# Seven block products for eight in the last chunk's second matrix product

## The chip, the cores and the metric

One core of one Trainium2 chip. The metric is the time of one execution on the device in microseconds (us), the median of several runs. PE is TensorE (its weight loads are shown as PEld), DVE VectorE, ACT ScalarE, POOL GpSimd, SP SyncE.

## The reference

An attention block with polynomial feature maps feeds a two-layer network with an exact GELU:

```python
def phi(x):                                   # r = 8, so 64 features
    a = np.einsum('rd,bhsd->bhsr', S1, x)
    b = np.einsum('rd,bhsd->bhsr', S2, x)
    return np.einsum('bhsi,bhsj->bhsij', a, b).reshape(*x.shape[:-1], r * r)
q_p, k_p = (phi(q), phi(k))                   # q, k, v: 4 batches, 4 heads, 1088 tokens, 32
kv = np.einsum('bhsf,bhsd->bhfd', k_p, v)
z = np.sum(k_p, axis=2)
num = np.einsum('bhsf,bhfd->bhsd', q_p, kv)
den = np.einsum('bhsf,bhf->bhs', q_p, z)[..., None] + 1e-06
x = (num / den).transpose(0, 2, 1, 3).reshape(4352, 128)
h = x @ w_in                                  # w_in: 128 x 2048
g = 0.5 * h * (1.0 + erf(h / np.sqrt(2)))
out = g @ w_out                               # w_out: 2048 x 128
```

All in float32.

## The kernel before

The 4352 tokens (4 batches of 1088) are cut into chunks. Each batch gives two chunks of 512 tokens, numbers 0 to 7; the 64 tokens that remain of each batch make a ninth chunk, number 8 (`NMAIN`), with 256 tokens. The hidden width 2048 is cut into 16 tiles of 128 (`fi`, `NF` = 16).

The program is one list of steps `(n, fi)`, numbered t. In each step `hidden(n, fi)` (L739) multiplies a tile of `w_in` with the chunk's `xT` into one of two banks `h_ps`, and ACT writes the GELU of it (L746) into a `block` tile in SBUF. The chunks 2 to 7 have 16 steps each, and chunk 8 has the last 16, t = 128 to 143. From t = 18 on a hidden product is issued as two matmuls of 64 output rows each, one for each half of the array (`by_halves`); for chunk 8 that holds to fi 4, and later tiles are one full matmul.

The second product, `g @ w_out`, runs some steps behind. For the main chunks it is done by pairs of tiles: with the 2x2 blocks of a pair (two tiles of hidden width by two halves of the tokens, and by two halves of the 128 output columns), seven block products take the place of eight. The block sums of `w_out` that this needs are made once (`channel_sums`, in tiles T[1] to T[4]); those of the tokens for each block of four tiles by POOL (`token_sums`, L790 to L793); the products are issued two at a time, one for each half of the array (`two_products`, L825); and `drain` (L837 to L846) and `combine` (L859, L860) add the seven sums up. `store` then transposes (L887) and writes the rows out by SP's queue.

For chunk 8 the second product has the other orientation: the tokens are the stationary operand, and the result has tokens as rows. `project` (L873) issues two matmuls of 128x128 for each tile, one for each half of its 256 tokens, and adds all 16 tiles up in two work banks (`w_ps`). The tiles fi 0 to 11 follow the hidden products from t = 133 on, two matmuls a step after the first few; the eight matmuls of fi 12 to 15 come last. Then DVE copies the first half and ACT the second (L882), and SP's and ACT's queues store them.

The order on each engine is that of the text: the program adds a dependency from every instruction to the one before it on its engine. What each step issues stands in tables by step: `slots[t]`, `products[t]`, `drains[t]` (the drain of chunk 7 at t = 133) and `done[t]` (its `combine` and `store` at t = 139). In one step the order is drains, hidden product, slots, stores, products.

Working tiles come from pools: "g" is a ring of four tiles of 128x512, free in the last steps; "sums" holds what `drain` writes; `out_bank()` gives one of two `o_ps` banks, in which chunk 7's seven products lie until its drain, `work_bank()` one of the `w_ps`.

Of the kernel before, what the change touches and what calls it, by code (L numbers as in the profile page):

```python
# [8 lines left out]
FP = mybir.dt.float32  # L9
# [7 lines left out]
def kernel(  # L17
# [18 lines left out]
    pe, dve, act, pool, sp = nc.tensor, nc.vector, nc.scalar, nc.gpsimd, nc.sync  # L36
    B, H, S, D = q.shape
# [4 lines left out]
    NF = d_ff // 128  # L42
# [5 lines left out]
    CW = JC * 128  # L48
    G = 128 // 32
    NCH = J // JC  # L50
    C = D + 1
    LAG = 2
    NMAIN = B * NCH
    NB = 4

    USUAL = 8
    NCHUNK = NMAIN + 1
    assert B == 4 and d_model == 128 == H * D == JC * D == 2 * F and H == 4 and REM == 64 and NCH == 2

    big = ctx.enter_context(tc.tile_pool(name="big", bufs=1))  # L60
    att = ctx.enter_context(tc.tile_pool(name="att", bufs=2))
    mlp = ctx.enter_context(tc.tile_pool(name="mlp", bufs=2))
# [8 lines left out]
    def work_bank():  # L71
        return work_banks()[:, 0]
# [7 lines left out]
    def out_bank():  # L80
        return ops.tile([128, CW], FP, name="o_ps")


    by_act, by_dve, by_pool = act.copy, dve.tensor_copy, pool.tensor_copy
# [12 lines left out]
    w_out_sb = [big.tile([128, c1 - c0], FP, name=f"w_out{i}") for i, (c0, c1) in enumerate(pieces)]  # L97
# [96 lines left out]
    for i, (queue, s) in enumerate(((act, S1), (sp, S2))):  # L194
        s, e = words(s)
# [528 lines left out]
    g_of, o_of = {}, {}  # L724

    def w_tile(w, fi):
        i = max(i for i, (c0, c1) in enumerate(pieces) if c0 <= fi * 128)
        at = fi * 128 - CUTS[i]
        return w[i][:, at:at + 128]
# [3 lines left out]
    def hidden(n, fi, by_halves=False):  # L733
        W = width[n]
        ps = first_banks.pop((n, fi)) if (n, fi) in first_banks else hidden_bank()
        w = w_tile(w_in_sb, fi)
        for rows in (slice(0, 64), slice(64, 128)) if by_halves else (slice(0, 128),):
            if (n, fi) not in begun:
                pe.matmul(ps[rows, :W], lhsT=w[:, rows], rhs=xT[n][:, :W], start=True, stop=True)  # L739
        if n < NCH and fi < USUAL:  # L740
            g_of[n, fi] = mlp.tile([128, CW], FP, name="g", bufs=4)
        else:
            if fi % NB == 0:
                blocks[n, fi // NB] = block(FP)
            g_of[n, fi] = blocks[n, fi // NB][:, fi % NB]
        act.activation(out=g_of[n, fi][:, :W], in_=ps[:, :W], func=ACT.Gelu)  # L746
# [13 lines left out]
    T = {}  # L760
# [94 lines left out]
    def combine(n):  # L855
# [6 lines left out]
            dve.tensor_add(out=N[:, 1], in0=N[:, 1], in1=usual[n])  # L862
        return N[:, 1]

    def project(n, fi, parts=range(B // 2), cols=slice(None)):
        first, final = fi == 0, fi == (USUAL if n < NCH else NF) - 1
        if first:
            o_of[n] = out_bank() if n < NMAIN else [work_bank() for i in range(B // 2)]
        g = g_of[n, fi]
        if n == NMAIN:  # L870

            for i in parts:
                pe.matmul(o_of[n][i][:, :128], lhsT=g[:, i * 128:(i + 1) * 128], rhs=w_tile(w_out_sb, fi),  # L873
                          start=first, stop=final)
            return
        pe.matmul(o_of[n][:, cols], lhsT=w_tile(w_out_sb, fi), rhs=g[:, cols], start=first, stop=final)  # L876

    def store(n):
        oT = mlp.tile([128, JC, d_model], FP, name="oT")
        if n == NMAIN:  # L880
            for i, copy, queue in ((0, by_dve, sp), (1, by_act, act)):
                copy(out=oT[:, i, :], in_=o_of[n][i][:, :128])  # L882
                queue.dma_start(out=out.rearrange("(two b s) d -> two b s d", two=2, s=S)[:, i, MAIN:S, :].rearrange("two s d -> s two d"),
                             in_=oT[:, i, :])
            return

        dve.transpose(out=oT.rearrange("p n d -> p (n d)"), in_=combine(n))  # L887
        row = n // NCH * S + n % NCH * CW
        if n < NCH:

            for c in range(d_model // 32):
                to = out[0:MAIN, c * 32:(c + 1) * 32].rearrange("(g t n j) d -> n j t g d", t=32, n=NCH, j=JC)[n]
                o = oT[c * 32:(c + 1) * 32].rearrange("p n (m d) -> p (n m) d", d=32)
                o = o.rearrange("p (g j) d -> j p g d" if n == 0 else "p (j g) d -> j p g d", j=JC)
                for j in range(JC):
                    sp.dma_start(out=to[j], in_=o[j])
            return
        to = out[row:row + CW].rearrange("(t n) d -> t n d", t=32)
        of = oT.rearrange("p n (m d) -> p (n m) d", d=32)
        for at in (slice(0, 16),) if n != NMAIN - 2 else (slice(0, 8), slice(8, 16)):  # L900
            for c in range(d_model // 32):
                sp.dma_start(out=to[:, at, c * 32:(c + 1) * 32], in_=of[c * 32:(c + 1) * 32, at])
# [250 lines left out]
    for t, (n, fi) in enumerate(steps):  # L1153
        if n < NCH and fi < USUAL:
            products[t + LAG].append((project, n, fi))
            if fi == USUAL - 1:
                slots[t + LAG + 1 + 2 * n].append(lambda n=n: take_usual(n))
        elif n == NMAIN:
            at_ = max(t + LAG, (n * NF + 5) if fi < 3 else (n * NF + 6) if fi < 5 else 0)
            if fi < NF - 4:  # L1160
                products[at_].append((project, n, fi))
            if fi == NF - 1:

                products[at_] += [(project, n, NF - f, (i,)) for f, i in ((4, 0), (3, 0), (2, 0), (4, 1), (1, 0), (3, 1),
                                                                          (2, 1), (1, 1))]
                done[at_ + 1].append(n)
        elif fi % NB == NB - 1:
            b = fi // NB
            opens = b == first_block(n)
            late = int(n < NCH or n == NCH and opens)  # L1170
            for later, pairs in ((3, 3), (4, 2), (5, 2)) if opens else ((2, 2), (3, 2), (4, 1), (5, 2)):
                later += late
                for i in range(pairs):
                    products[t + later].append((two_products, n, b, len([p for q in products.values() for p in q
                                                                        if p[:3] == (two_products, n, b)])))
            if b == NF // NB - 1:
                drains[t + 6 + late].append(n)
                done[t + 12].append(n)

    for t in range(len(steps) + LAG):  # L1180
        if t < 4:

            hidden(0, t)
            if t == 0:
                expand_multiply(1, 0)
                w_out[0].fields()
                expand_copy(1, 1)
                expand_multiply(1, 1)
            if t == 1:
                w_out[0].low_words()  # L1190
                w_out[0].exponents()
                w_out[0].finish()
                w_out[1].fields()
            if t == 2:
                w_out[1].low_words()
            if t == 3:
                banks = work_banks()
                numerators_by_token(1, halves(banks), range(JC))
                w_out[1].mantissas(by_pool=True)
                w_out[1].exponents()  # L1200
                divide(1, halves(banks), 0)
                w_out[1].signs()
                w_out[1].product()
                project(0, 0)
                project(0, 1, cols=slice(0, 256))
                turn_half(1, 0, work_bank(), by_act)
                project(0, 1, cols=slice(256, 512))
                turn_half(1, 1, work_bank(), by_dve)
            continue
        if t == 4:  # L1210
            first_hidden(1, 0)
            for f, *a in products[t]:
                f(*a)
            first_hidden(1, 1)
        for n in drains[t]:
            drain(n)
        sooner = t == NMAIN * NF
        if sooner:
            for f, *a in products[t]:
                f(*a)  # L1220
        if t < len(steps):
            n, fi = steps[t]
            hidden(n, fi, by_halves=t >= 18 and (n < NMAIN or fi < 5))
        if t < len(steps) and steps[t][0] < NMAIN and steps[t][1] % NB == NB - 1:
            n, b = steps[t][0], steps[t][1] // NB
            if b >= first_block(n):
                token_sums(n, b)
        for f in slots[t]:
            f()
        for n in done[t]:  # L1230
            store(n)
        if t != 4 and not sooner:
            for f, *a in products[t]:
                f(*a)
# [41 lines left out]
```

## Time and profile before

| | us |
|---|---|
| median of 3 runs | 258.85 (258.77 to 259.4) |
| profiled execution, its own time | 258.97 |
| profiled execution, span from first to last instruction | 257.2 |
| PE busy | 253.0 |
| POOL / DVE / ACT busy | 164.5 / 151.6 / 114.7 |

The page gives busy time and share of each engine, the span in 40 slices, the chain of work that ended last, and the costliest groups of instructions. In the lines of a timeline the columns are start in us, duration in us, engine, line of the kernel, operation, output<-inputs, shape (for PE `128*64` is the size of the stationary operand, rows by columns, and what follows is the moving one), and xN for N merged records; idle time ahead of it and what ended that stand in brackets. A float32 matmul shows as two records. The granted TensorE clock is 1.00 throughout.

### The profile page before, as it was taken

The page shows a single profiled execution, that of the slowest core. Times are in us where ns is not written, and L with a number is a line of the kernel's source. Part 1 is how long each engine was busy: PE and PEld are TensorE (multiplying, and loading weights), DVE is VectorE, ACT ScalarE, POOL GpSimd, SP SyncE. Part 2 cuts the span into 40 slices and gives each one's busy share as a digit, 9 for nine tenths or more (in the row PEclk, how much of TensorE's full clock was granted, in tenths as well). Part 3 has the DMA queues.
Part 4 walks back from the last instruction along what each step waited for, and adds up shares of the span by engine and source line. Part 5 has one row for each costly group of instructions (what it writes and reads, how often), then busy time and mean ns, then how long its engine had stood idle before and what let it go on. Part 6 is the DMA issues. An engine that isn't in the chain of part 4 may idle for free.

```text
span 257.2 us, 5633 instructions
## 1 busy us (share of the span) xinstructions
PE 253.0 (98%) x2265; PEld 133.4 (52%) x2265; DVE 151.6 (59%) x314; ACT 114.7 (45%) x222; POOL 164.5 (64%) x175
## 2 busy tenths in 40 slices
PE   8999999999999999999999999999999999999995
PEld 4856444255444545454444455445544444445794
DVE  4896888969698987580278976399307000700330
ACT  3784767533535333533335332623444334433442
POOL 3414007799968787587758774787758777877300
PEclk9999999999999999999999999999999999999999
DMA  6699558710001101102000001000200200020020
GB/s 205 176 320 307 146 128 205 198 17 9 0 0 18 26 4 23 20 10 33 0 3 0 0 15 31 1 4 0 34 10 11 33 0 4 9 32 3 0 41 23
DMA packets 29082, 13.48 MB, mean 52 GB/s; under 512 B 21888, under 2 KB 27264, under 8 KB 29056
## 3 DMA queue, kind: packets, MB, share of 16 engines
q1 hardware_dynamic: 28624, 12.79, 20.2%
q8 instruction: 18, 0.29, 0.5%
q10 hardware_dynamic: 432, 0.33, 0.4%
q14 instruction: 8, 0.07, 0.1%
HBM read 10.88 MB, written 2.23 MB: 51 GB/s over the span
## 4 chain that ended last, share of the span: by engine, by line
PE 98%; ACT 0%; issue 0%
PE h_ps L739 45%; PE o_ps L825 33%; PE o_ps L876 5%; PE w_ps L873 3%; PE w_ps L455 1%; PE w_ps L603 1%; PE w_ps L658 1%; PE w_ps L908 1%; PE w_ps L569 1%; PE h_ps L755 1%; PE h_ps L347 1%; PE o_ps L444 1%; PE w_ps L994 1%; PE w_ps L684 0%; PE o_ps L396 0%; PE w_ps L485 0%
## 5 line engine op out<-in xcount | busy, mean ns | idle before, releaser
L739 PE MATMUL h_ps<-xT,w_in 128*64 128x512 f32 (+3 forms) x514 | 137.0, 576 | 0.0
L746 ACT ACTIVATE block<-h_ps 128x512 f32<-128x512 f32 (+1 forms) x128 | 73.0, 571 | 117.3 <-PE h_ps L739 115.3
L739 PEld LDWEIGHTS h_ps<-xT,w_in 128*64 128x64 f32 (+1 forms) x514 | 41.8, 142 | 30.6 <-issue 11.6
L825 PE MATMUL o_ps<-block,w_out 128*64 128x256 f32 x224 | 57.5, 379 | 0.0
L790 POOL TENSOR_TENSOR bits_low<-block 128x512 f32<-128x512 f32 x28 | 36.1, 1291 | 27.2 <-ACT block L746 27.2
L825 PEld LDWEIGHTS o_ps<-block,w_out 128*64 128x64 f32 x224 | 30.5, 137 | 38.0 <-issue 27.5
L791 POOL TENSOR_TENSOR bits_a<-block 128x512 f32<-128x512 f32 x28 | 35.8, 1277 | 11.7 <-ACT block L746 11.6
L840 DVE COPY sums<-o_ps 64x256 f32<-64x256 f32 x8 | 3.3, 416 | 60.6 <-PE o_ps L825 60.6
L792 POOL TENSOR_TENSOR bits_e<-bits_a,block 128x512 f32<-128x512 f32 x28 | 36.0, 1287 | 2.2
L793 POOL TENSOR_TENSOR bits_m<-block,bits_e 128x512 f32<-128x512 f32 x28 | 36.0, 1286 | 2.2
L825 PE MATMUL o_ps<-bits_a,small 128*64 128x256 f32 x112 | 28.8, 379 | 0.0
L825 PE MATMUL o_ps<-block,small 128*64 128x256 f32 x112 | 28.8, 379 | 0.0
L825 PE MATMUL o_ps<-bits_low,small 128*64 128x256 f32 x112 | 28.8, 379 | 0.0
L825 PE MATMUL o_ps<-bits_m,w_out 128*64 128x256 f32 x112 | 28.7, 379 | 0.0
L825 PEld LDWEIGHTS o_ps<-block,small 128*64 128x64 f32 x112 | 15.2, 137 | 17.9 <-issue 10.8
L825 PE MATMUL o_ps<-bits_e,small 128*64 128x256 f32 x112 | 17.1, 383 | 0.0
L876 PE MATMUL o_ps<-g,w_out 128*128 128x512 f32 (+1 forms) x34 | 16.5, 572 | 0.0
L825 PEld LDWEIGHTS o_ps<-bits_m,w_out 128*64 128x64 f32 x112 | 15.3, 137 | 0.0
L825 PEld LDWEIGHTS o_ps<-bits_a,small 128*64 128x64 f32 x112 | 15.2, 137 | 0.0
L825 PEld LDWEIGHTS o_ps<-bits_low,small 128*64 128x64 f32 x112 | 15.2, 137 | 0.0
L615 DVE STREAM_TRANSPOSE w_ps<-w_ps 128x512 f32<-128x512 f32 (+1 forms) x7 | 4.8, 688 | 17.1 <-ACT xT L669 12.7
L825 PEld LDWEIGHTS o_ps<-bits_e,small 128*64 128x64 f32 x112 | 7.7, 137 | 10.6 <-issue 8.8
(201 smaller groups left out, 302.6 us busy)
## 6 DMA issues: line engine op xcount, KB each, us to landing
block<-in_moe_w_in_dram SPq DMA_DIRECT2D x3, 512.0 KB, 10.3
block<-in_moe_w_out_dram SPq DMA_DIRECT2D x3, 512.0 KB, 10.4
k<-in_k_dram SPq DMA_DIRECT2D x12, 128.0 KB, 2.7
v<-in_v_dram SPq DMA_DIRECT2D x12, 128.0 KB, 3.2
q<-in_q_dram SPq DMA_DIRECT2D x24, 64.0 KB, 2.5
out_dram<-oT SPq DMA_DIRECT2D x21, 64.0 KB, 2.2
q_first<-in_q_dram SPq DMA_DIRECT2D x2, 256.0 KB, 4.2
v<-in_v_dram SPq DMA_DIRECT2D x2, 256.0 KB, 4.8
```

The costliest lines, as they stand in the source:

```text
L347: pe.transpose(ps[:, i * 128:(i + 1) * 128], in_=s, identity=ident)
L615: dve.transpose(out=tok, in_=ps[:, :, :H2])
L739: pe.matmul(ps[rows, :W], lhsT=w[:, rows], rhs=xT[n][:, :W], start=True, stop=True)
L746: act.activation(out=g_of[n, fi][:, :W], in_=ps[:, :W], func=ACT.Gelu)
L790: pool.tensor_sub(out=s[3], in0=a11, in1=a21)
L791: pool.tensor_add(out=s[1], in0=a21, in1=a22)
L792: pool.tensor_sub(out=s[2], in0=s[1], in1=a11)
L793: pool.tensor_sub(out=s[4], in0=a12, in1=s[2])
L825: pe.matmul(acc[n][bank][half * 64:(half + 1) * 64, col:col + HW], lhsT=fixed, rhs=moving, start=opens and e == 0 and name in "4715", stop ...
L840: dve.tensor_copy(out=N[lo, 0, one], in_=a0[lo, one])
L873: pe.matmul(o_of[n][i][:, :128], lhsT=g[:, i * 128:(i + 1) * 128], rhs=w_tile(w_out_sb, fi), start=first, stop=final)
L876: pe.matmul(o_of[n][:, cols], lhsT=w_tile(w_out_sb, fi), rhs=g[:, cols], start=first, stop=final)
```

## The change

In the ninth chunk the second product of the tiles fi 0 to 11 (`BLOCKED` = 12 of 16) is done by seven block products for eight, by pairs k = 0 to 5 of tiles. `sums_rem` makes four token sums of 128x128 for each pair, on POOL for k = 0 to 3 and on DVE for 4 and 5; the order is s[2], s[0], s[1], s[3], of which the third and the fourth each read the one before. `product_rem` issues one block product as two matmuls, each with 64 tokens stationary and 64 columns moving; all seven, over all pairs, are added up side by side in one work bank. The 42 products are spread over the steps t = 133 to 143, in each pair in the order 4, 1, 2, 7, 5, 6, 3, of which 7, 5, 6 and 3 use the token sums. `combine_rem` adds the seven up with seven DVE operations behind the last of them. The tiles fi 12 to 15 go as before, with full 128x128 matmuls, but start fresh sums in two `o_ps` banks, and DVE adds those to what `combine_rem` left, where before DVE and ACT copied. All hidden products of the chunk are now issued in halves. The `combine` and `store` of chunk 7 move from t = 139 to t = 136. The sums use the "g" ring.

```diff
     USUAL = 8
+    BLOCKED = 12
...
+    ORDER_REM = "4127563"
+    COLS_REM = {name: slice(i * 64, (i + 1) * 64) for i, name in enumerate("1267543")}
+
+    def sums_rem(k):
+        g = [g_of[NMAIN, 2 * k + i][:, :256].rearrange("p (half x) -> p half x", half=2) for i in range(2)]
+        (a11, a21), (a12, a22) = ([a[:, h] for h in range(2)] for a in g)
+        s = mlp.tile([128, CW], FP, name="g", bufs=4).rearrange("p (j x) -> p j x", j=4)
+        eng = dve if k > 3 else pool
+        eng.tensor_sub(out=s[:, 2], in0=a11, in1=a21)
+        eng.tensor_add(out=s[:, 0], in0=a21, in1=a22)
+        eng.tensor_sub(out=s[:, 1], in0=s[:, 0], in1=a11)
+        eng.tensor_sub(out=s[:, 3], in0=a12, in1=s[:, 1])
+        sums[NMAIN, k] = s
+
+    def product_rem(k, name):
+        if k == 0 and name == ORDER_REM[0]:
+            acc[NMAIN] = work_bank()
+        s = sums[NMAIN, k]
+        if name in "12":
+            fi = 2 * k + int(name) - 1
+            tokens, fixed = g_of[NMAIN, fi][:, 0:128], w_tile(w_out_sb, fi)[:, 0:64]
+        elif name == "3":
+            tokens, fixed = s[:, 3], w_tile(w_out_sb, 2 * k + 1)[:, 64:128]
+        elif name == "4":
+            tokens, fixed = g_of[NMAIN, 2 * k + 1][:, 128:256], T[4][:, k]
+        else:
+            j = "567".index(name)
+            tokens, fixed = s[:, j], T[j + 1][:, k]
+        for i in range(2):
+            rows = slice(i * 64, (i + 1) * 64)
+            pe.matmul(acc[NMAIN][rows, COLS_REM[name]], lhsT=tokens[:, rows], rhs=fixed,
+                      start=k == 0 and name == ORDER_REM[0], stop=k == BLOCKED // 2 - 1, skip_group_check=True)
+
+    def combine_rem():
+        p = acc[NMAIN][:, :7 * 64].rearrange("p (k d) -> p k d", d=64)
+        to, u = (att.tile([128, 2, CW], FP, name="sums")[:, 0] for i in range(2))
...
+        dve.tensor_copy(out=u[:, 0], in_=p[:, 0])
+        dve.tensor_add(out=u[:, 1:3], in0=p[:, 1:3], in1=u[:, 0:1].broadcast_to(two))
+        dve.tensor_add(out=u[:, 3:5], in0=p[:, 3:5], in1=u[:, 2:3].broadcast_to(two))
+        dve.tensor_copy(out=to[:, 0, 0], in_=u[:, 1])
+        dve.tensor_add(out=to[:, 0, 1], in0=p[:, 6], in1=u[:, 4])
+        dve.tensor_add(out=to[:, 1, 1], in0=p[:, 4], in1=u[:, 3])
+        dve.tensor_add(out=to[:, 1, 0], in0=p[:, 5], in1=u[:, 3])
+        drained[NMAIN] = to
+
     def project(n, fi, parts=range(B // 2), cols=slice(None)):
-        first, final = fi == 0, fi == (USUAL if n < NCH else NF) - 1
-        if first:
-            o_of[n] = out_bank() if n < NMAIN else [work_bank() for i in range(B // 2)]
+        first, final = fi == (BLOCKED if n == NMAIN else 0), fi == (USUAL if n < NCH else NF) - 1
+        if first and n not in o_of:
+            o_of[n] = out_bank() if n < NMAIN else [out_bank() for i in range(B // 2)]
...
-            for i, copy, queue in ((0, by_dve, sp), (1, by_act, act)):
-                copy(out=oT[:, i, :], in_=o_of[n][i][:, :128])
+            for i, queue in ((0, sp), (1, act)):
+                dve.tensor_add(out=oT[:, i, :], in0=o_of[n][i][:, :128], in1=drained[n][:, i].rearrange("p c d -> p (c d)"))
...
         elif n == NMAIN:
-            at_ = max(t + LAG, (n * NF + 5) if fi < 3 else (n * NF + 6) if fi < 5 else 0)
-            if fi < NF - 4:
-                products[at_].append((project, n, fi))
+            if fi % 2 and fi < BLOCKED:
+                slots[t].append(lambda k=fi // 2: sums_rem(k))
+            at_ = t + LAG
             if fi == NF - 1:
+
+                names = [(k, name) for k in range(BLOCKED // 2) for name in ORDER_REM]
+                steps_rem = NF - 5
+                for i, (k, name) in enumerate(names):
+                    products[n * NF + 5 + i * steps_rem // len(names)].append((product_rem, k, name))
+                products[n * NF + 4 + steps_rem].append((combine_rem,))
...
-                done[t + 12].append(n)
+                done[t + (12 if n < NMAIN - 1 else 9)].append(n)
...
-            hidden(n, fi, by_halves=t >= 18 and (n < NMAIN or fi < 5))
+            hidden(n, fi, by_halves=t >= 18)
```

More of the change, by code (lines that the diff above doesn't have):

```diff
@@ new lines, in combine_rem @@
+    def combine_rem():
+        p = acc[NMAIN][:, :7 * 64].rearrange("p (k d) -> p k d", d=64)
+        to, u = (att.tile([128, 2, CW], FP, name="sums")[:, 0] for i in range(2))
+        to = to[:, :256].rearrange("p (half c d) -> p half c d", half=2, c=2)
+        u = u[:, :320].rearrange("p (k d) -> p k d", k=5)
+        two = [128, 2, 64]
+        dve.tensor_copy(out=u[:, 0], in_=p[:, 0])
[6 more added lines that the diff above has]
+        drained[NMAIN] = to
```

## The prediction

> **What bounds the kernel now.** I read the page first (busy shares, slices, the chain that ended last), then the timeline of the last 20 us on all engines, then the rows elsewhere in the trace whose shapes the change will use.
>
> ```profile
> span 257.2 us, 5633 instructions
> PE 253.0 (98%) x2265; PEld 133.4 (52%) x2265; DVE 151.6 (59%) x314; ACT 114.7 (45%) x222; POOL 164.5 (64%) x175
> PE 98%; ACT 0%; issue 0%
> 240.00:257.20 17.20, 14.01 (x104) 12.41 (x100) 4.79 (x11) 6.23 (x16) 0.15 (x1) 1.00 0.13 24
> ```
>
> TensorE (PE) is the chain: 98% of the span, and no other engine has a share to speak of. The last line is a stretch of the windows view (PE, PEld, DVE, ACT, POOL busy, then clock 1.00): from 240 us on VectorE and GpSimd are nearly free, and PE is busy to about 254.0. What the change alters lies entirely there. Up to the step of fi 5 of the remaining tokens (t=133) the instruction lists of the two kernels agree, engine by engine.
>
> ```profile
> 240.03 0.60 PE L825 MATMUL o_ps<-bits_e,small 128*64 128x256 f32 x4
> 240.46 0.60 PE L739 MATMUL h_ps<-xT,w_in 128*64 128x256 f32 x4
> 240.68 0.14 PEld L825 LDWEIGHTS o_ps<-block,w_out 128*64 128x64 f32 x1
> 240.89 0.38 PE L825 MATMUL o_ps<-block,w_out 128*64 128x256 f32 x1
> 241.54 0.38 PE L825 MATMUL o_ps<-bits_m,w_out 128*64 128x256 f32 x1
> 241.85 0.70 PE L739 MATMUL h_ps<-xT,w_in 128*128 128x256 f32 x2
> 249.44 0.60 PE L739 MATMUL h_ps<-xT,w_in 128*128 128x256 f32 x2
> 250.32 0.60 PE L739 MATMUL h_ps<-xT,w_in 128*128 128x256 f32 x2
> 252.06 1.95 PE L873 MATMUL w_ps<-w_out,block 128*128 128x128 f32 x16
> 254.05 0.27 ACT L882 COPY oT<-w_ps 128x128 f32<-128x128 f32 x1 [1.40 <-PE w_ps L873]
> 254.34 0.64 ACTq L883 DMA_DIRECT2D out_dram<-oT  x1
> ```
>
> Each fp32 matmul is two records (the eight last products are the 16 at 252.06). To read: a hidden product of this chunk in halves takes 0.43 us (240.46 to 240.89), two pairs of 256 columns also 0.43 (240.03 to 240.46), so a pair of half-width records 0.215. A step of the tail is 0.88 (249.44 to 250.32): one hidden product and two second products, PE without a gap. From 241.85 to 252.06 PE does the 11 hidden products of fi 5 to 15 and the 24 second products of fi 0 to 11: 10.21 us. Call 252.06 T0: from there run the eight last products (fi 12 to 15, 1.95 us), the copy 0.27, the store's issue at T0+2.28, and 2.86 us to the end of the span.
>
> **PE work removed and added.** Away go 24 matmuls of 128x128, in come 6 x 7 = 42 products of 64 columns, each as two half-width matmuls, so four records.
>
> ```profile
> 6.49 0.64 PE L396 MATMUL h_ps<-S,kT 128*64 128x64 f32 x16
> 5.97 0.69 PE L396 MATMUL o_ps<-S,kT 128*64 128x64 f32 x16 [0.24 <-ACT kT L349]
> L396 PE MATMUL h_ps<-S,kT x16: 222/222/222, 6.5 to 6.9; 128*64 128x64 f32 x16
> 97.08 1.08 PE L455 MATMUL w_ps<-k_p,v 128*32 128x64 f32 x64
> 97.98 0.29 PE L455 MATMUL w_ps<-k_p_rem,v_rem_aug 128*32 128x64 f32 x8
> ```
>
> L396 has exactly the new shape, two 64-wide halves in turn, 64 columns, new weights each time. Of its 0.64 us the last record is 0.22, so 15 intervals take 0.42: 0.028 per record, 0.112 per product. L455 agrees in quarters: 64 records in 0.90 us, 0.056 for four side by side, 0.112 for two passes. From below, a quarter of the 256-column pair gives 0.0537 a pass, 0.107 a product. From above, the first 16 of L396 with their start took 0.52 (5.97 to 6.49): 0.13. I take 0.112, the price of both rows that run on without a start.
>
> In half mode PE goes on at 241.54 + 0.215 = 241.76. The switch to full width, which now comes there (0.31 from 241.54 to 241.85 in place of 0.215), moves behind the products: 0.10. New T0 = 241.76 + 11 x 0.43 + 42 x 0.112 + 0.10 = 241.76 + 4.73 + 4.70 + 0.10 = 251.29, which is **0.77 us sooner**; with 0.107 it is 0.98, with 0.13 nothing. By columns alone the saving would be 24 x 0.215 - 42 x 0.107 = 0.67; the rest is the tail's full-width steps, 0.88 where 0.86 would do. That all hidden products are now in halves is in this sum.
>
> **The token sums on GpSimd and VectorE.** 16 subtractions and additions of 128x128 go to POOL (pairs 0 to 3), 8 to DVE (4, 5). Three of seven products wait for none of them; the other four each carry a wait, and PE runs in order, so a late sum holds up every hidden product behind it.
>
> ```profile
> 238.88 1.28 POOL L793 TENSOR_TENSOR bits_m<-block,bits_e 128x512 f32<-128x512 f32 x1
> 66.82 0.45 POOL L777 TENSOR_TENSOR small<-w_out 128x128 f32<-128x128 f32 x1
> 67.24 0.45 POOL L778 TENSOR_TENSOR small<-w_out 128x128 f32<-128x128 f32 x1
> 67.65 0.45 POOL L779 TENSOR_TENSOR small<-w_out,small 128x128 f32<-128x128 f32 x1
> 68.18 0.47 POOL L780 TENSOR_TENSOR small<-w_out,small 128x128 f32<-128x128 f32 x1
> ```
>
> POOL is free at 240.16. One operation is 0.45, the next starts 0.42 later, or 0.53 later if it reads the one before. The order in `sums_rem` is two free ones and two that read, so 0.42 + 0.53 + 0.53 + 0.42 = 1.90 a pair; the third sum is ready 1.40 after its pair's start, the fourth 1.93. Tightest is pair 3: its start is 240.16 + 3 x 1.90 = 245.86, sums at 247.26 and 247.79. PE reaches step 139 after 6 hidden products and 23 second ones, 241.76 + 2.58 + 2.58 = 246.92; product "6" of pair 3 is its fourth, at 246.92 + 0.43 + 0.34 = 247.69, "3" comes at 248.23. Weights are loaded 0.21 ahead (240.68 to 240.89), so the slack is 0.22 and 0.23. Earlier pairs have more; without company no stall. But there is company:
>
> ```profile
> 245.02 0.42 DVE L859 TENSOR_TENSOR sums<-sums 64x256 f32<-64x256 f32 x1
> 245.45 0.42 DVE L860 TENSOR_TENSOR sums<-sums 64x256 f32<-64x256 f32 x1
> 245.90 0.71 DVE L887 STREAM_TRANSPOSE oT<-sums 128x512 f32<-128x512 f32 x1
> 93.98 1.55 POOL L793 TENSOR_TENSOR bits_m<-block,bits_e 128x512 f32<-128x512 f32 x1
> 94.02 0.37 DVE L859 TENSOR_TENSOR sums<-sums 64x256 f32<-64x256 f32 x1
> 149.89 1.34 POOL L793 TENSOR_TENSOR bits_m<-block,bits_e 128x512 f32<-128x512 f32 x1
> 149.02 1.06 DVE L859 TENSOR_TENSOR sums<-sums 64x256 f32<-64x256 f32 x1
> ```
>
> L859 and L860 read both operands from SBUF, as do the new DVE sums. Beside POOL such an operation takes 1.06 in place of 0.42, and POOL's takes 1.34 or 1.55 in place of 1.28: POOL loses 0.06 to 0.27 each time. In the last stretch L859 and L860 meet POOL twice (0.12 to 0.54), and some three of the DVE sums of pair 4, from 246.6 on and half as long, meet its last ones (0.1 to 0.4). POOL is late by 0.2 to 0.95, PE stalls 0 to 0.7: I take **0.30**, a lateness of 0.5 less the slack. DVE itself, later by up to 0.45 for each of L859 and L860 as it waits for a POOL operation, ends the transpose by 247.5 and pair 4's sums by 248.8. They are wanted from 248.9 to 249.2, so nothing further is late.
>
> The Trainium skill, page "SBUF — State Buffer", section "Who interferes with whom", says that a VectorE operation with two SBUF inputs and a GpSimd one that reads SBUF exclude each other, the later one waiting for the whole instruction of the other. The trace agrees in kind, and in size shows POOL losing 0.27 to L859's 0.37.
>
> **Combining and storing.** `combine_rem` puts seven DVE operations behind the last of the 42 products, beside the last eight, and both final copies become DVE additions.
>
> ```profile
> 156.53 0.23 DVE L621 COPY q_ac<-w_ps 128x64 f32<-128x64 f32 x1
> 156.79 0.23 DVE L622 TENSOR_TENSOR q_ac<-w_ps,q_ac 128x64 f32<-128x64 f32 x1
> 70.26 0.29 DVE L621 COPY q_ac<-w_ps 128x128 f32<-128x128 f32 x1
> 70.59 0.29 DVE L622 TENSOR_TENSOR q_ac<-w_ps,q_ac 128x128 f32<-128x128 f32 x1
> 67.06 0.41 DVE L842 TENSOR_TENSOR sums<-o_ps,sums 64x256 f32<-64x256 f32 x1
> 67.39 0.84 DVE L844 TENSOR_TENSOR sums<-o_ps,sums 64x256 f32<-64x256 f32 x2
> ```
>
> An operation on 64 columns that reads the one before follows in 0.26, on 128 in 0.33; one that need not wait starts 0.08 before the end of the other (67.39 against 67.47). The first can start at new T0 - 0.13 + 0.22 + 0.04 = T0+0.13 (last product's start, its length, the signal as from 254.01 to 254.05). With all in a row: five at 0.26 and two at 0.33 make 1.96, the two additions 0.33 and 0.29, issue 0.02: T0+2.73, 0.45 later than now. With the independent ones overlapped the chain is some 0.45 shorter, and then the last product sets the end: T0 + 1.99 + 0.29 + 0.02 = 2.30, 0.02 later. I take **0.10**, since four of the seven need not wait. Beyond the additions the stores are the same.
>
> Three edits come to nothing. Storing the last whole chunk sooner moves nothing in its queue: L859 already starts right behind the drain (245.02), and on DVE and SP its place stays the same; it only keeps pair 4's sums behind it. The output banks are last read by that drain, which ends before 245.02, 6 us ahead of their new use. ACT loses a copy of 0.27 on the path, counted above.
>
> **Sum.** -0.77 + 0.30 + 0.10 = -0.37 on the profiled execution's 258.97 us (span 257.2 and 1.77 outside it): 258.60. That run lies 0.12 above the median of 258.85, so **258.5**. About 0.3% (0.78 us) is what a measurement of this kernel can tell from no change.
>
> **Rivals.** *All covered* (0.34): POOL stays within its slack and the adds overlap; -0.77 + 0.02 at the price taken, -0.96 at 0.107: 258.1 to 257.9, across the edge of the bound, 0.26 of it beyond. For it: PE's records of the shape run at the price without a gap. Against: L859 has to pass a busy POOL here.
>
> *The end stands alone* (0.10): the DVE chain runs without overlap, 0.45, and the stall stays at 0.30: -0.02, 258.8. For it: the two L844 take 0.84 for 2 x 0.41, so they did not overlap though independent.
>
> *POOL's sums are late* (0.13), the slower side: each of the six DVE operations that meet POOL (L859, L860 at 0.42, four sums at 0.29) holds it for its whole length: 2 x 0.42 + 4 x 0.29 = 2.0 us, less 0.22 slack a stall of 1.8 at step 139. -0.77 + 1.8 + 0.1 = +1.1: 260.0. It decides against the change from a lateness of 0.9 on (stall 0.67). For it: 94.02, where POOL lost 0.27; against: 149.02, where it lost 0.06. It is also what the SBUF page's rule, named above, would make of it.
>
> *A small matmul costs a fixed time* (0.03): 64 columns take as long as 128, 0.107 a pass for two halves side by side, 0.215 a product, 42 x 0.215 = 9.03 in place of 4.70: +4.3 - 0.37: 262.8. Halves that did not run side by side would cost the same. L396 and L455 speak against both. The Trainium skill's "TensorEngine Tiling (Array Packing)", section "Instruction Overhead", warns of this: about 60 cycles for each matmul, so that one should not tile a dimension that is already small. L396's 0.028 us per 64-column record does not show it.
>
> My own case has 0.40 and runs from 258.1 to 258.85. Faster 0.26 (from all covered), same 0.58 (its other 0.08, mine and the bare end), slower 0.16. The range takes in all covered and the lower part of late sums: 257.9 to 259.5.
>
> **What would show it.** Right: 168 records at 0.028 each, all L739 halves in the tail at 0.43, the eight last products starting near 251.3 to 251.6, PE idle 0.1 to 0.5 us at steps 139 and 140 behind POOL, the last addition within 0.1 of the last product's end plus 0.29. Wrong: PE idle of a microsecond behind POOL or DVE; records at 0.05; a DVE chain that ends 0.4 us after the last product; a new gap before the hidden products.

## The result, and the profile after

The changed kernel takes 258.38 us (median of 22 runs, 257.91 to 258.86) against 258.88 of the kernel before (22 runs, 258.52 to 259.4): a ratio of 0.998, 95% interval 0.9973 to 0.9986. That is 0.50 us less; 258.5 was forecast. The difference lies within the 0.3% that the forecast called no change, but its interval is clear of 1. The profiled execution of one experiment below (e1) ran at a granted clock of 0.85, so only its timed runs are used, and its profile was taken again as e8.

The first lines of the page after, then PE's timeline at the tail's start, in a middle step and at the end (columns as in the prediction; L740 is now the hidden product, L896 the seven-for-eight products, L922 the last eight):

```profile
span 256.1 us, 5952 instructions
PE 251.9 (98%) x2407; PEld 131.5 (51%) x2407; DVE 156.0 (61%) x330; ACT 114.5 (45%) x221; POOL 171.7 (67%) x191
PE 98%; ACT 0%; DVE 0%; issue 0%
239.82 0.60 PE L740 MATMUL h_ps<-xT,w_in 128*64 128x256 f32 x4
241.12 0.60 PE L740 MATMUL h_ps<-xT,w_in 128*64 128x256 f32 x4
...
242.01 0.60 PE L740 MATMUL h_ps<-xT,w_in 128*64 128x256 f32 x4
242.45 0.40 PE L896 MATMUL w_ps<-small,g 128*64 128x64 f32 x8
242.68 0.29 PE L896 MATMUL w_ps<-w_out,g 128*64 128x64 f32 x4
242.79 0.29 PE L896 MATMUL w_ps<-small,block 128*64 128x64 f32 x4
242.91 0.60 PE L740 MATMUL h_ps<-xT,w_in 128*64 128x256 f32 x4
...
250.65 0.29 PE L896 MATMUL w_ps<-w_out,g 128*64 128x64 f32 x4
250.86 2.05 PE L922 MATMUL o_ps<-w_out,block 128*128 128x128 f32 x16
```

PE is still the chain. The two spans differ by 1.1 us, but that must not be read as the gain: fi 4's hidden product, up to which PE runs the same instructions in both kernels, starts at 240.46 before and at 239.82 after. (The prediction says that up to t = 133 the lists agree engine by engine. POOL's do not: its first sums are issued at t = 129 and run from 239.47 on. The products that read them come after 241.55.) So 0.64 of the 1.1 arose ahead of the change and is a difference between executions; in the changed kernel's second profile (e9) the same product starts at 240.14. What the change did is read from that mark on. I cut the stretch at T0, the start of the last eight products, and at the issue of ACT's last store, and call the time from the mark to the end of the span the tail:

| kernel | mark to T0 | T0 to issue | mark to issue | tail |
|---|---|---|---|---|
| before | 11.60 | 2.28 | 13.88 | 16.74 |
| forecast | 11.13 | 2.38 | 13.51 | 16.37 |
| changed | 11.04 | 2.42 | 13.46 | 16.28 |
| e9, changed again | 11.04 | 2.41 | 13.45 | 16.26 |
| e8, halves, eight products | 11.28 | 2.26 | 13.54 | 16.38 |
| e2, only hidden products in halves | 14.61 | 2.38 | 16.99 | 19.79 |
| e3, no token sums | 11.04 | 2.41 | 13.45 | 16.29 |
| e4, all sums on POOL | 11.67 | 2.41 | 14.08 | 16.89 |
| e5, last eight in halves | 10.94 | 2.29 | 13.23 | 16.08 |
| e10, e5 again | 10.94 | 2.29 | 13.23 | 16.07 |
| e6, 14 of 16 tiles | 12.06 | 2.01 | 14.07 | 16.98 |
| e7, store late | 11.04 | 2.41 | 13.45 | 16.80 |

Each row is worked out from the starts in that kernel's PE and ACT timelines and its span. The span is printed to 0.1 only, so a tail may be off by 0.05 and a difference of two tails by 0.1. I read differences from "mark to issue", which repeats to 0.01 (13.46 and 13.45, 13.23 and 13.23). From the issue to the end of the span it is 2.8 to 2.9 in every kernel but e7, where SP's store comes last. By this column the change gained 0.42.

POOL and DVE in the same stretch of the changed kernel, from their timelines:

```profile
244.74 0.52 POOL L877 TENSOR_TENSOR g<-block,g 128x128 f32<-128x128 f32 x1
245.22 0.64 POOL L874 TENSOR_TENSOR g<-block 128x128 f32<-128x128 f32 x1
246.36 0.46 POOL L876 TENSOR_TENSOR g<-g,block 128x128 f32<-128x128 f32 x1
246.89 0.46 POOL L877 TENSOR_TENSOR g<-block,g 128x128 f32<-128x128 f32 x1
244.38 0.56 DVE L860 TENSOR_TENSOR sums<-sums 64x256 f32<-64x256 f32 x1
244.96 0.59 DVE L861 TENSOR_TENSOR sums<-sums 64x256 f32<-64x256 f32 x1
246.38 0.58 DVE L875 TENSOR_TENSOR g<-block 128x128 f32<-128x128 f32 x1
247.53 0.29 DVE L877 TENSOR_TENSOR g<-block,g 128x128 f32<-128x128 f32 x1
250.98 0.23 DVE L905 COPY sums<-w_ps 128x64 f32<-128x64 f32 x1 [2.10 <-PE w_ps L896]
252.16 0.21 DVE L911 TENSOR_TENSOR sums<-w_ps,sums 128x64 f32<-128x64 f32 x1
252.37 0.29 DVE L931 TENSOR_TENSOR oT<-o_ps,sums 128x128 f32<-128x128 f32 x1
252.95 0.29 DVE L931 TENSOR_TENSOR oT<-o_ps,sums 128x128 f32<-128x128 f32 x1 [0.29 <-PE o_ps L922]
253.28 0.65 ACTq L932 DMA_DIRECT2D out_dram<-oT  x1
```

POOL's sums are nearly undisturbed: only two of the 16 took longer than 0.46, beside L860 and L861. At the end DVE is idle for 0.29 before the second addition: the combining is hidden, and PE's last product sets the end.

### The profile page after: what moved, and what is told of

It reads as the page before. It is cut to its first block, busy times and chain, and to the rows that moved or that the text cites. A ratio compares the mean times of both kernels' runs of the same rounds, so it can differ in the third digit from the quotient of the medians.

```text
span 256.1 us, 5952 instructions
## 1 busy us (share of the span) xinstructions
PE 251.9 (98%) x2407; PEld 131.5 (51%) x2407; DVE 156.0 (61%) x330; ACT 114.5 (45%) x221; POOL 171.7 (67%) x191
## 4 chain that ended last, share of the span: by engine, by line
PE 98%; ACT 0%; DVE 0%; issue 0%
PE h_ps L740 45%; PE o_ps L826 33%; PE o_ps L925 5%; PE w_ps L896 2%; PE w_ps L456 1%; PE w_ps L604 1%; PE w_ps L659 1%; PE w_ps L957 1%; PE w_ps L570 1%; PE o_ps L922 1%; PE h_ps L756 1%; PE o_ps L445 1%; PE w_ps L1043 1%; PE h_ps L348 1%; PE w_ps L685 0%; PE o_ps L397 0%
## 5 line engine op out<-in xcount | busy, mean ns | idle before, releaser
L740 PE MATMUL h_ps<-xT,w_in 128*64 128x512 f32 (+2 forms) x536 | 137.1, 568 | 0.0
L740 PEld LDWEIGHTS h_ps<-xT,w_in 128*64 128x64 f32 (+1 forms) x536 | 40.7, 140 | 30.3 <-issue 11.6
```

## The experiments

The open question was where the 0.42 us comes from: from seven products for eight, from leaving full width, or from less than that with something given back. Ratios are to the kernel before, run beside each.

**e1 and e8: all in halves, still eight products.** The kernel before, with two edits:

```diff
-            hidden(n, fi, by_halves=t >= 18 and (n < NMAIN or fi < 5))
+            hidden(n, fi, by_halves=t >= 18)
...
-                pe.matmul(o_of[n][i][:, :128], lhsT=g[:, i * 128:(i + 1) * 128], rhs=w_tile(w_out_sb, fi),
-                          start=first, stop=final)
+                for rows in (slice(0, 64), slice(64, 128)):
+                    pe.matmul(o_of[n][i][rows, :128], lhsT=g[:, i * 128:(i + 1) * 128][:, rows], rhs=w_tile(w_out_sb, fi),
+                              start=first, stop=final)
```

> The kernel before, with every matmul of the last chunk's tail issued as two 64-wide halves (hidden products and second products), but still eight products for eight and the old copies at the end. Tail means the time from the start of the hidden product of fi 4 to the end of the span: 16.74 us before (257.2 - 240.46), 16.28 after the change (256.1 - 239.82). Theory 1: a good part of the gain is that the array no longer changes between half and full width. Then 11 x 0.435 + 24 x 0.215 = 9.95 take the place of 10.21 from 241.85, the start is 0.09 sooner, and the last eight take 0.06 less: tail 16.3 to 16.35, as good as the whole change. Theory 2: the gain is the seventh saved of the products. Then halves alone give nothing: tail 16.7.

> The same kernel as the first of the earlier ones (all in halves, eight products for eight, old copies at the end), whose profiled execution ran at a clock of 0.85 and so has no tail to compare; its ratio to the kernel before was 0.9983. Theory 1 (half width alone gives nearly all of the gain): tail 16.3 to 16.35, a step of the tail 0.86. Theory 2 (the ratio hid a difference from run to run): tail 16.5 or more.

Ratio 0.9983 (0.9974 to 0.9993), and again 0.9987 (0.9978 to 0.9996). PE's timeline of e8, a step and the last eight:

```profile
248.43 0.60 PE L739 MATMUL h_ps<-xT,w_in 128*64 128x256 f32 x4
248.86 0.61 PE L874 MATMUL w_ps<-w_out,block 128*64 128x128 f32 x8
249.30 0.60 PE L739 MATMUL h_ps<-xT,w_in 128*64 128x256 f32 x4
251.90 1.92 PE L874 MATMUL w_ps<-w_out,block 128*64 128x128 f32 x32
```

A step is 0.87 in place of 0.88, the first change of width is gone (0.31 from the record at 241.54 to the one at 241.85, and there 0.70 for two records that otherwise take 0.60), and the last eight are quicker. The issue comes 0.34 sooner than before, with not one product saved; the tail, 16.38, lies just above theory 1's 16.3 to 16.35 and well below theory 2's. So the larger part of what the change gained is to be had from the width alone.

**e2: only the hidden products in halves.** The first of the two edits alone.

> The kernel before, with all hidden products of the last chunk in halves and the second products full as they were, so that the array changes width twice in nearly every step. Theory 1: a change of width costs 0.2 us each time (the first full record of the last eight shows 0.10 of it ahead and 0.10 within); 10 to 11 steps with two changes each: tail longer by 2 to 4.4 us, 18.7 to 21.1. Theory 2 (a change costs only what the gap shows once, 0.1, or nothing): tail 16.7 to 17.8.

Ratio 1.0127 (1.0111 to 1.0142), tail 19.79, within theory 1's range.

```profile
248.61 0.65 PE L739 MATMUL h_ps<-xT,w_in 128*64 128x256 f32 x4
249.19 0.71 PE L873 MATMUL w_ps<-w_out,block 128*128 128x128 f32 x4
249.83 0.65 PE L739 MATMUL h_ps<-xT,w_in 128*64 128x256 f32 x4
248.61 0.20 PEld L739 LDWEIGHTS h_ps<-xT,w_in 128*64 128x64 f32 x4
249.19 0.52 PEld L873 LDWEIGHTS w_ps<-w_out,block 128*128 128x128 f32 x4 [0.39 <-issue]
PEld w_ps L873 <- issue: 3.8, 10, 0.4
```

The same work in steps of 1.22 (248.61 to 249.83) in place of 0.87: two changes of width, one each way, cost 0.35, so 0.17 to 0.18 each on average. The weight loads show where it hides: the first one behind each change starts with its matmul (248.61, 249.19) and not ahead of it, and the last line, of the waits, counts ten waits for "issue", 3.8 us in all and 0.4 at most, ahead of the full-width loads. In e8, without changes, the loads start 0.11 and 0.21 ahead of the matmuls at 248.43 and 248.86. What the profile calls a busy PE holds these gaps. The prediction had 0.10 for a change.

**e3: no token sums.** Leaves the sums out; products 3, 5, 6, 7 take blocks of g in their place.

```diff
-        s = mlp.tile([128, CW], FP, name="g", bufs=4).rearrange("p (j x) -> p j x", j=4)
-        eng = dve if k > 3 else pool
-        eng.tensor_sub(out=s[:, 2], in0=a11, in1=a21)
...
-        sums[NMAIN, k] = s
+        sums[NMAIN, k] = [a11, a21, a12, a22]
```

> The changed kernel without the token sums: the products 3, 5, 6, 7 take blocks of g in their place, so no operation of POOL or DVE makes sums and PE waits for none. Theory 1: no sum was late, and a wait that is fulfilled costs nothing: tail 16.28 within 0.05, product 0.115 to 0.117. Theory 2: waits and weight loads behind them are what makes a product 0.116 in place of 0.112: 42 x 0.004 = 0.17 less, tail 16.1. Theory 3: the meeting of POOL and DVE holds something up that the trace does not show: less still.

Ratio 0.9974 (0.9964 to 0.9984), tail 16.29, as theory 1 had it; a step of four products is 0.90 as before:

```profile
247.57 0.60 PE L740 MATMUL h_ps<-xT,w_in 128*64 128x256 f32 x4
248.47 0.60 PE L740 MATMUL h_ps<-xT,w_in 128*64 128x256 f32 x4
```

So the 24 sums and the waits for them cost PE nothing, and a product costs 0.116 with or without them.

**e4: all sums on POOL.**

```diff
-        eng = dve if k > 3 else pool
+        eng = pool
```

> The changed kernel with the sums of pairs 4 and 5 on POOL too. POOL's pair takes 1.9 us; pair 3 ended at 247.35 in the changed kernel's trace (11.25 after its tail's mark), so pair 4's fourth sum comes at 249.26 and is wanted at about 248.8, and pair 5's at 251.2, wanted at 250.85 plus the first delay. Theory 1: a late sum holds PE up one for one: PE waits 0.4 to 0.5 for pair 4 and as much again for pair 5: tail 17.0 to 17.2, slower than before by 0.3 to 0.5. Theory 2 (PE has other work or more slack): tail 16.3.

Ratio 1.0007 (0.9998 to 1.0016), tail 16.89; the issue comes 0.62 later than in the changed kernel, and 0.7 to 0.9 was expected.

```profile
249.10 0.46 POOL L877 TENSOR_TENSOR g<-block,g 128x128 f32<-128x128 f32 x1
248.47 0.60 PE L740 MATMUL h_ps<-xT,w_in 128*64 128x256 f32 x4
249.61 0.34 PE L896 MATMUL w_ps<-w_out,g 128*64 128x64 f32 x4 [0.19 <-POOL g L877]
249.78 0.60 PE L740 MATMUL h_ps<-xT,w_in 128*64 128x256 f32 x4
250.67 0.60 PE L740 MATMUL h_ps<-xT,w_in 128*64 128x256 f32 x4
251.78 2.05 PE L922 MATMUL o_ps<-w_out,block 128*128 128x128 f32 x16
```

Pair 4's fourth sum ends at 249.56, product "3" starts at 249.61, and that step lasts 1.31 (248.47 to 249.78) instead of 0.90. From 250.67 to T0 it is 1.11 instead of 0.88. This is what the rival of the late sums counts on, here from too much work on POOL and not from DVE holding it: a late sum is paid by everything behind it, 0.41 and 0.23, the whole gain and a little more. The wait that the timeline prints is only 0.19 of the 0.41; the rest lies inside time that it counts as busy (the product after the wait takes 0.34 where others take 0.29, and the record before the wait is printed as 0.22 long, though the next one otherwise starts 0.029 after it).

**e5 and e10: the last eight in halves too.** The second edit of e1, made to the changed kernel.

> The changed kernel with the last eight products (fi 12 to 15) in halves too, so that the array never changes width in the tail. Theory 1 (a change of width costs 0.20, full 128-column records 0.005 each over half ones, and the DVE chain has 0.29 of slack): the last eight start 0.10 sooner and take 1.89 in place of 2.05, the second addition follows 0.27 sooner: tail 16.0 in place of 16.28, ratio to the kernel before about 0.997. Theory 2 (the DVE chain bounds the end): no more than 0.05 sooner, tail 16.25.

> The changed kernel itself once more, beside the next one on the same chip, so that the two can be set against the same runs of the kernel before. Tail 16.28 as in its first profile, ratio 0.998.

> The changed kernel with the last eight products in halves, again. Theory 1 (the tails of 16.08 and 16.28 are what tells the two apart, the rest of the span is alike): tail 16.08 and a median 0.2 us below that of the changed kernel beside it. Theory 2 (the difference lay in the stretch ahead of the tail): medians alike.

Ratio 0.9972 (0.9962 to 0.9981), and again 0.9972 (0.9963 to 0.9981) beside the changed kernel's 0.9979 (0.997 to 0.9988); medians 258.10 and 258.30. Mark to issue 13.23 twice, against 13.46 and 13.45.

```profile
251.04 0.29 PE L896 MATMUL w_ps<-w_out,g 128*64 128x64 f32 x4
251.16 1.92 PE L923 MATMUL o_ps<-w_out,block 128*64 128x128 f32 x32
252.76 0.66 DVE L932 TENSOR_TENSOR oT<-o_ps,sums 128x128 f32<-128x128 f32 x2
```

The last eight follow the last product after 0.12 in place of 0.21 and take 1.92 in place of 2.05; the DVE additions now stand nearly back to back (0.66 for two of 0.29). This version is the fastest; its intervals overlap those of the changed kernel, so it is these two pairs, 0.22 to 0.23 apart, that tell them apart. Of the 0.27 expected 0.04 is missing, most of it since the last eight take 1.92 and not 1.89. It is still PE that sets the end: its last product ends at 253.08 (251.16 + 1.92), and the second addition starts at 253.13, when DVE has been idle for 0.08.

**e6: 14 of 16 tiles.** `BLOCKED = 14`, and only fi 14 and 15 left for the end.

> The changed kernel with 14 of the 16 tiles by seven products, so that only four products are left behind the combining. Theory 1 (the eight last products of 2.05 us are what hides the 1.39 us of DVE work before the additions): seven more products add 0.81 to the end of the seven-for-eight part, and from there the DVE chain sets the end, 0.25 + 1.39 + 0.20 + 0.29 against 0.13 + 2.05 + 0.29 now: 0.4 slower than the changed kernel, tail 16.7. Theory 2 (more seven for eight is more gain, the chain is hidden anyway): PE's work is 0.05 less, tail 16.2.

Ratio 1.0006 (0.9997 to 1.0014), tail 16.98; the issue comes 0.61 later than in the changed kernel, and 0.4 was expected.

```profile
252.68 1.16 PE L922 MATMUL o_ps<-w_out,block 128*128 128x128 f32 x8
254.17 0.49 DVE L931 TENSOR_TENSOR oT<-o_ps,sums 128x128 f32<-128x128 f32 x2
254.69 0.63 ACTq L932 DMA_DIRECT2D out_dram<-oT  x1
247.17 0.46 POOL L876 TENSOR_TENSOR g<-g,block 128x128 f32<-128x128 f32 x1
247.30 0.72 PE L896 MATMUL w_ps<-small,g 128*64 128x64 f32 x12
```

T0 to issue is 0.41 shorter (2.01), where theory 1 had 0.34: PE is done at 253.84, and DVE adds until 254.66, so its chain sets the end. T0 itself is 1.02 later and not 0.81: with 49 products in the same steps PE comes to pair 3 sooner, and the products 7, 5 and 6 of it take 0.72 where they otherwise take 0.52, since POOL's third sum ends only at 247.63.

**e7: the store of chunk 7 late again.** `done[t + 12]` for all chunks.

> The changed kernel with the combine and store of chunk 7 back at t = 139, behind the DVE sums of pairs 4 and 5 in DVE's order. Theory 1 (the move is off the path): tail 16.28 to 16.35; the store's transpose comes some 4 us later, at about 250, and DVE is free again when the seven products are done at 250.9. Theory 2 (the late store stands in the way of the last stores on SP's queue or of the combining on DVE): tail longer by 0.2 or more.

Ratio 0.9997 (0.9987 to 1.0006): the gain is gone. Tail 16.80, and theory 2 holds. The lines of e7; the fifth is a line of its DMA queues from 251.43 to 253.18 (packets, MB, share), and the last one, for comparison, is of the changed kernel:

```profile
250.07 0.71 DVE L936 STREAM_TRANSPOSE oT<-sums 128x512 f32<-128x512 f32 x1
250.81 3.71 SPq L951 DMA_DIRECT2D out_dram<-oT  x4
251.43 1.75 SPq L951 DMA_DIRECT2D out_dram<-oT  x1
254.62 0.60 SPq L932 DMA_DIRECT2D out_dram<-oT  x1
q8 instruction: 1, 0.02, 4.3%
254.15 0.63 ACTq L932 DMA_DIRECT2D out_dram<-oT  x1
246.32 2.59 SPq L951 DMA_DIRECT2D out_dram<-oT  x4
```

T0 and ACT's store are where they were. But the transpose waits on DVE behind the sums, the four stores of chunk 7 keep SP's queue until 254.52, and SP's own last store goes out at 254.62, 1.1 after its data (the first addition ends at 253.53). In the changed kernel the four are issued from 246.32 on and SP's last at 252.69. The sums ahead of the store are not the whole of it. With four issues in 2.59 as there, SP would have been free at 253.40, ahead of its data. The missing 1.1 is one issue, the second, which takes 1.75 where the other three take 0.58 to 0.63, and one transfer that the view calls "instruction" falls into it (at 251.5; in the changed kernel it comes at 250.5, when SP issues nothing). The only other issue of L951 above 0.7 in e7 (1.70, at 184.47) has such a transfer just ahead of it, at 184.2. Whether that is the reason no run here shows.

## Why the prediction was right, by its steps

The forecast of -0.37 on the profiled execution stands against -0.42 from the mark to the issue and -0.50 in the medians (0.36 to 0.70 by the interval). All three terms of the sum were mis-sized: PE's work by +0.21, the stall by -0.30, the end by +0.04. That the first two nearly cancel is luck. The mechanism that the runs show, no stall and an overlapped chain, is that of the rival "all covered", whose number (-0.75 and more) failed by the same price of a product; its condition held, and the forecast's own case needed a stall behind POOL that never came.

**PE work, -0.77 forecast, -0.56 measured.** The step that failed is the price of a product, 0.112 from L396 and L455. From 241.12 to 250.86 PE took 9.74: less 11 hidden products at 0.435 and 0.10 ahead of T0 it leaves 4.86 for 42 products, 0.116 each. That is 0.16 of the 0.21 missed; the other 0.05 is the hidden product, 0.435 where 0.43 was taken. e3 shows that the waits are not the cause. Why these records run at 0.029 and L396's at 0.028 stays open.

**What that gain consists of.** The prediction put 0.67 on columns saved and the rest on full-width steps. That took the columns at 0.107 a product where the sum took 0.112; at 0.112 they are worth 24 x 0.215 - 42 x 0.112 = 0.46, and the width the other 0.31. e8 and e5 divide it so: halves alone give 0.34, seven for eight on top of that 0.31 (13.54 to 13.23). At 0.116 a product and 0.216 a second product, as in e8, the columns are worth 24 x 0.216 - 42 x 0.116 = 0.31, which agrees. The changed kernel gives back 0.23 by going to full width for the last eight, 0.10 ahead of T0 and 0.13 within them.

**The stall, 0.30 forecast, none measured.** POOL was late by 0.2 and not 0.5 (pair 3's third sum 7.00 after the mark, 6.80 worked out): L860 and L861 cost it 0.06 and 0.18, but the DVE sums of pair 4 cost it nothing; it was DVE that waited (0.58 for an operation of 0.28). PE came 0.1 later to pair 3 than worked out, so that 0.1 of the slack was left. That a late sum is paid by all that stands behind it is what e4 shows, so the rival of the late sums had the price right and the condition wrong: POOL was not held for the whole length of each DVE operation. The Trainium skill, page "SBUF — State Buffer", section "Who interferes with whom", has the later of the two wait for the whole instruction of the other. The trace agrees in that one side waits, DVE more often than POOL, but not in the size: the DVE operation at 246.38 ended at 246.96, 0.14 after POOL's that began at 246.36, though it takes 0.28 by itself.

**The end, 0.10 forecast, 0.14 measured, for another reason.** The DVE chain overlapped as in the better of the two cases (its last four operations start 0.12 to 0.14 apart) and left DVE idle for 0.29. What cost the time is the change of width, 0.17 to 0.20 where the prediction had 0.10: the second half of it lies within the first record of the last eight. The Trainium skill, page "TensorEngine Tiling (Array Packing)", section "Key Properties", says that changing the tiling mode drains the engine; e2 shows what a change costs here, 0.17 to 0.18, though not that a drain is what it consists of.

**The store three steps sooner, nothing forecast.** Against the kernel before that holds, its place in the queues is the same. But the prediction did not say what it costs if it is not done, and e7 shows 0.5 us: the whole gain. Of the other rivals, the bare end did not come: the chain overlaps in e6 too, where with only four products left to hide it, it does set the end. The fixed cost of a small matmul is out: 168 records took 4.86 us and not 9.

## What to carry to other kernels

Before an algebraic saving on the array is credited, make the kernel that changes only its form (here, halves without the saved product): it gave 0.34 of the 0.42. Keep one width through a stretch of small matmuls, and look for the gaps in start-to-start times, since a busy PE hides them. When new work is put on an in-order engine, look at what already stands in that queue and which transfer waits for it: a store that used to be free cost 0.5 us once sums stood ahead of it and one slow issue came on top. And add up a forecast's terms one by one against the trace: here the total was right while two terms were wrong by 0.2 and 0.3.

## What the runs showed of the hardware

A change between half and full width of the array costs 0.17 to 0.18 us on average of the two directions (e2: 1.22 a step with two of them, 0.87 with none). Half-width float32 records of 64 columns follow each other in 0.029 us, 6% over the 0.0272 that a quarter of the 0.109 for 256 columns makes (a hidden product of 0.435 is four such records). Each of chunk 7's four stores of 64 KB takes SP's queue 0.58 to 0.63 us to issue (2.59 for the four), but one in e7 took 1.75; it is the one into which an "instruction" transfer fell.
